# Merged stores of the x parts, and weight preparation and attention issued in other steps, in a linear-attention and two-MoE kernel

## The chip, the cores and the metric

One core of a Trainium2 chip runs the whole program in one launch. The metric is device time in microseconds (us), the median of three runs. The engines are named as in the profile: PE (TensorE; its weight loads are PEld), DVE (VectorE), ACT (ScalarE), POOL (GpSimd) and SP (SyncE), which here only issues transfers.

## What is computed

All data are float32. `B, H, S, D = 4, 8, 576, 64`; there are 2304 tokens and the model width is 512.

```python
kv = einsum('bhsd,bhse->bhde', k, v)
o = einsum('bhsd,bhde->bhse', q, kv)
o = o / sqrt(mean(o * o, -1) + 1e-06) * g_norm
x = o.transpose(0, 2, 1, 3).reshape(2304, 512)
h = x @ moe_w_in                      # 512 x 2048
x = (h * sigmoid(h)) @ moe_w_out      # 2048 x 512
a, b = x @ moe2_w_a, x @ moe2_w_b     # 512 x 1536 each
out = (a * b) @ moe2_w_out            # 1536 x 512
```

## The kernel before

**Numbers.** A matrix that goes into TensorE is split into a high part, which is a cast on ACT, and a low part, source minus high, on DVE (`halve`, L436). A product is three matmuls: high by high, high by low, low by high.

**Blocks and visits.** Tokens are worked in six blocks of 384 (`TB`), so a moving tile is 128x384. The list `VISITS` (L42) gives the first MoE layer its order: the hidden tiles (16 per block) are passed through in nine visits. Visits 0 to 4 take blocks 0 and 1 in plain steps, one hidden tile each, numbered g = 0 to 31. A plain step multiplies into a bank `hp`, has ACT apply the gate (L418) and the cast `gh` (L364), DVE the low part `gl` (L369), and then multiplies the hidden tile of the step before into the four output banks `x1p` (L380). After that come the side jobs of the step: `at(g, ...)` enters one, `at(-g, ...)` one between gate and low part, `soon` one before the gate's step.

**Units.** Blocks 2 and 3, and later 4 and 5, are worked in pairs by a scheme of seven products in place of eight (`PRODUCTS`, L51; `seven`, L661): the x of the two blocks is combined into seven parts, `X_PARTS` = B11, T2, T3, B21, T1, T4, B22, and the weights into seven combinations. Visits 5 and 7 are eight such units each (`unit`, L803); a unit makes four hidden tiles, forms its sums `u` (L678, L681) and `h` (L827) on DVE from the banks X_h, Y_h, V_h and Z_h, and has two `x1_mm` of earlier tiles in it. `at_unit(b, u, n, ...)` hangs a side job behind product n of unit u. Visits 6 and 8 (16 steps each, from `P2A` = g 48 and from `base[8]` = g 80) only multiply the second block's stored hidden tiles into the output banks: casts `gh`, low parts `gl` and 12 matmuls per step. Then 18 iterations of the same kind make the second MoE layer.

**Preparation.** `combine` (L449) makes the seven parts of x for a pair of blocks and one kt, with high and low part of each; for the second layer they go to `xcd` in DRAM, high and low by one store each, from half pages of [128, 384] (`half_page`), the blocks having been loaded by `last_blocks` (L1007) into two pages. `prepare` (L497) does the same for one pair of matrices of w_a or w_b: `load`; `scale` (two ACT operations, L305); `first_half` and `second_half` (decoding, L311, L317, L324 on DVE, and the cast of `a`); `add` (the low part of `a`, then four sums s1, s3, s2, s4, L545 to L548); `high` (casts of `s_0`, `s_1` and `m`, L437); `low` (their low parts, L438). `flush` then gives the stores to `wd` to SP. Twelve pairs (n = 0 to 11, w_a and w_b in turn) are spread over the units of blocks 2 and 4, the last over visit 8.

**Order.** The order in which the program issues is the order in which each engine works; an instruction that waits holds all that is behind it on its engine. SP issues every transfer, also in order. Most tiles are of one size and rotate through 37 buffers, the pages (`NPAGE`), so a new tile waits for the last use of an earlier one.

**Attention.** For blocks 2 and 3, `kv_pair` and `attend` are entered by the table at L925 to L935: `turn_q` transposes (L159, DVE), `stage_b` (L220, PE), the norm, and `stage_f` into `xf` (L915, ACT).

```python
for f, h in zip(steps, (0, 1, 2, 5, 5, 7)):
    at_unit(*slot(b, h0 + h), f)
```

Of the kernel before, what the change touches and what calls it, by code (L numbers as in the profile page):

```python
# [8 lines left out]
F32 = mybir.dt.float32  # L9
F32R = mybir.dt.float32r  # L10
# [50 lines left out]
def tile_linattn_moe_moe2(ctx: ExitStack, tc: tile.TileContext, q, k, v, g_norm,  # L61
                          w_in, w_out, w_a, w_b, w_out2, out):
    nc = tc.nc
    B, H, S, D = q.shape
# [28 lines left out]
    def page(shape, dt, name):  # L93
        return sb.tile(shape, dt, tag="page", bufs=NPAGE, name=name)
# [4 lines left out]
    def mid(shape, dt, name):  # L99
        return sb.tile(shape, dt, tag="mid", bufs=5, name=name)  # L100
# [245 lines left out]
    acc, part, gg = {}, {}, {}  # L346
# [88 lines left out]
    def halve(hi, lo, src, *stores):  # L435

        return (lambda: nc.scalar.copy(hi, src),  # L437
                lambda: nc.vector.tensor_sub(lo, src, hi.bitcast(F32)),  # L438
                *[lambda to=to, t=t: nc.sync.dma_start(to, t.bitcast(F32)) for to, t in stores])
# [9 lines left out]
    def combine(d, kt, place, blocks=None, keep=None, home=None):  # L449

        st, wait = {}, {}

        def new(name):
            st[name] = place([P, TB], F32, f"{name}_{d}_{kt}")
            return st[name]

        def get():
            for n in range(2):  # L460
                for r in range(2):
                    st[f"B{r + 1}{n + 1}"] = (blocks or (lambda n, r: part[2 * d + n][:, 2 * r + kt, :]))(n, r)

        def hi(name):
            h = home(name, f"h{name}_{d}_{kt}") if home else place([P, TB], F32R, f"h{name}_{d}_{kt}")
            low = home(name, f"l{name}_{d}_{kt}") if home else st[name].bitcast(F32R)
            i = X_PARTS.index(name)
            if keep is None:
                to = xcd[d, i, :, :, kt, :]
                first_, *wait[name] = halve(h, low, st[name], (to[:, 0], h), (to[:, 1], low))  # L470
            else:
                keep[i, 0, kt], keep[i, 1, kt] = h, low
                first_, *wait[name] = halve(h, low, st[name])
            first_()

        def lo(name):
            rest, *put_ = wait.pop(name)
            rest()
            if blocks:
                stores.extend(put_)  # L480
            else:
                for f in put_:
                    f()

        def sub(to, of, by, into=None):
            t = st[into] if into else place([P, TB], F32, f"{to}_{d}_{kt}")
            nc.vector.tensor_sub(t, st[of], st[by])
            st[to] = t

        return [(get, lambda: hi("B11"), lambda: sub("T1", "B12", "B11")), (lambda: hi("T1"), lambda: lo("B11")),  # L490
                (lambda: sub("T3", "B22", "B12", "B12"),), (lambda: hi("T3"), lambda: sub("T2", "B22", "T1")),
                (lambda: hi("B22"), lambda: lo("T1")), (lambda: hi("T2"), lambda: lo("T3")),
                (lambda: lo("B22"),), (lambda: sub("T4", "B21", "T2"),),
                (lambda: hi("B21"), lambda: lo("T2")), (lambda: hi("T4"), lambda: lo("B21")),
                (lambda: lo("T4"),), ()]
# [286 lines left out]
    hw, hx, xf, g1 = {}, {2: {}, 4: {}}, {}, {}  # L782
# [103 lines left out]
    base = []  # L886
    n = 0
# [5 lines left out]
    def at(g, fn, *args):  # L893
        side.setdefault(g, []).append(lambda: fn(*args))
# [27 lines left out]
    def at_unit(b, u, n, fn, *args):  # L922
        inner.setdefault((b, u, n), []).append(lambda: fn(*args))

    for b, g0s in ((2, (12, 14, 16, 18)), (3, (20, 22, 24, 26))):  # L925
        at(g0s[0] - 4, load_kvt, b)
        for g0, p in zip(g0s, (0, 2, 1, 3)):
            at(g0 - 3, load_kv, b, p)
            at(g0, kv_pair, b, p)
    for (j, p), g0 in zip([(2, 0), (2, 2), (3, 0), (3, 2), (2, 1), (2, 3), (3, 1), (3, 3)],  # L930
                          (12, 14, 16, 18, 20, 22, 24, 25)):
        at(g0 - 5, load_q_blocks, j, p)
        at(g0 - 2, turn_q, j, p)
        at(g0, attend, j, p)
        at(-(g0 + 1), norm_mul, j, p)  # L935
        at(g0 + 3, stage_f, j, p)

    P2A = base[6]
# [15 lines left out]
    def half_page(shape, dt, name):  # L954

        if not halves:
            t = page([P, 2, TB], F32R, name)
            halves.extend((t[:, 1], t[:, 0]))
        t = halves.pop()
        return t if dt == F32R else t.bitcast(dt)  # L960

    def home(part_, name):

        if part_ == "B11":
            return first.tile([P, TB], F32R, tag="qb", bufs=4, name=name)
        return half_page([P, TB], F32R, name)

    def x_parts(b, kt, places):
        todo = []

        def parts(n):
            if not todo:
                todo.extend(combine(f"h{b}", kt, mid, lambda n, r: xf[b, 2 * r + kt][:, n], hx[b], home))
            for f in todo[n]:
                f()

        for n, g in enumerate(places):
            at(g, parts, n)
# [10 lines left out]
    def slot(b, h):  # L989
        return (b,) + divmod(min(h, 7 * NF1 // 2 - 1), 7)  # L990

    for n in range(2 * NPAIR):
        load, steps = prepare(("wa", "wb")[n % 2], n // 2, n <= 7)
        if n == 2 * NPAIR - 1:
            at_unit(4, 7, 3, load)
            for i, f in enumerate(steps):
                at(base[8] + 1 + i, f)
            continue
        b, h0 = (2, 7 * (n + 2)) if n < 3 else (4, 7 * (n - 3))
        if h0 == 0:  # L1000
            at(P2A + 14, load)
        else:
            at_unit(*slot(b, h0 - 5), load)
        for f, h in zip(steps, (0, 1, 2, 5, 5, 7)):
            at_unit(*slot(b, h0 + h), f)

    def last_blocks(d, kt):  # L1007

        t = [page([P, 2, TB], F32, f"b_{kt}_{r}") for r in range(2)]
        for r in range(2):  # L1010
            for n in range(2):
                nc.sync.dma_start(t[r][:, n], x1d[2 * d + n, :, 2 * r + kt, :])
        return lambda n, r: t[r][:, n]

    for i in range(3):
        at(P2A + i, lambda: put())
    for u in (5, 6, 7):
        for n in range(7):
# [1 line left out]
    for kt in range(2):  # L1020
        todo = []

        def blocks0(kt=kt, todo=todo):
            todo.extend(combine(0, kt, half_page, last_blocks(0, kt)))

        def parts0(n, todo=todo):
            for f in todo[n]:
                f()

        at_unit(2, 5 + kt, 6, blocks0)  # L1030
        for n in range(12):
            at_unit(2, 6 + kt, 1 + n // 2, parts0, n)

    made = {}

# [8 lines left out]
    for u in range(6):  # L1044
        g0 = (7, 10, 14, 18, 22, 25)[u]
# [165 lines left out]
    with tc.manual_schedule():  # L1211
# [63 lines left out]
        todo, late = [], {}  # L1275
        for n, (d, p) in enumerate(seq):
            new = 0 < n < NPAIR
            m = n % NPAIR
            if 1 <= m <= 4 and n < 2 * NPAIR:

                kt, h = divmod(m - 1, 2)
                if h == 0:
                    late[kt] = combine(d + 1, kt, half_page, late.pop("blocks"))
                todo = late[kt][6 * h:6 * h + 6]
            products(d, p, (lambda: x1_mm(*prev)) if n == 0 else None,
                     decode_out(p, 0) if 0 < n < NPAIR else [])
            if n % NPAIR == NPAIR - 1 and n + 1 < len(seq):
                for i in range(7):
                    load_x(d + 1, i)
            free_pairs(n, False)  # L1290
            load_pairs()
            if n > 0:
                more = [(f,) for f in decode_out(p, 1)] if new else []
                if todo:
                    more = [(tuple(more[i]) if more else ()) + tuple(todo[i]) for i in range(6)]
                out_mm(n - 1, more)
                todo = []
                free_pairs(n - 1, True)
# [36 lines left out]
```

## Time and profile before

| | |
|---|---|
| runs, us | 868.41, 868.54, 867.34; median 868.41 |
| the profiled execution, us | 866.76; its span 865.0 |
| PE busy | 850.8 us, 98% of the span |
| PEld | 807.4 us, 93% |
| DVE | 622.2 us, 72% |
| ACT | 347.8 us, 40% |
| POOL | 52.6 us, 6% |
| bytes over the span | 230.03 MB, 266 GB/s |

All stages are PE work with other engines beside it, so the table says only that the time is PE's. What a change of order does is read where PE waits, on the time line of that place. Matmuls are pipelined: a row that gives 1.20 us for six matmuls of 384 columns is followed by the next 1.04 us after its start, and an instruction of DVE or ACT likewise overlaps the next by 0.05 to 0.1 us. The distance of two starts is therefore the price of an instruction, and its duration the time until others can use its result.

### The profile page before, as it was taken

The page shows a single profiled execution, that of the slowest core. Times are in us where ns is not written, and L with a number is a line of the kernel's source. Part 1 is how long each engine was busy: PE and PEld are TensorE (multiplying, and loading weights), DVE is VectorE, ACT ScalarE, POOL GpSimd, SP SyncE. Part 2 cuts the span into 40 slices and gives each one's busy share as a digit, 9 for nine tenths or more (in the row PEclk, how much of TensorE's full clock was granted, in tenths as well). Part 3 has the DMA queues.
Part 4 walks back from the last instruction along what each step waited for, and adds up shares of the span by engine and source line. Part 5 has one row for each costly group of instructions (what it writes and reads, how often), then busy time and mean ns, then how long its engine had stood idle before and what let it go on. Part 6 is the DMA issues. An engine that isn't in the chain of part 4 may idle for free.

```text
span 865.0 us, 13734 instructions
## 1 busy us (share of the span) xinstructions
PE 850.8 (98%) x4966; PEld 807.4 (93%) x4967; DVE 622.2 (72%) x1191; ACT 347.8 (40%) x708; POOL 52.6 (6%) x73
## 2 busy tenths in 40 slices
PE   7999999999999999999999999999999999999998
PEld 5799999999998999999999999999999999999996
DVE  4879989777956779989746788876576665545555
ACT  4666765544545456556522533221412211221110
POOL 5430111100000500000000000000000000000000
PEclk9999999999999999999999999999999999999999
DMA  9985886189986659999999998496688475755001
GB/s 276 372 222 160 258 244 234 66 312 405 408 315 183 190 218 336 405 404 385 369 405 417 388 336 333 152 379 242 238 305 276 135 292 200 292 219 195 1 0 74
DMA packets 127972, 230.03 MB, mean 266 GB/s; under 512 B 41504, under 2 KB 87072, under 8 KB 127904
## 3 DMA queue, kind: packets, MB, share of 16 engines
q1 hardware_dynamic: 127904, 229.15, 73.7%
q8 instruction: 39, 0.64, 0.3%
q14 instruction: 29, 0.24, 0.1%
HBM read 160.17 MB, written 68.94 MB: 265 GB/s over the span
## 4 chain that ended last, share of the span: by engine, by line
PE 83%; DMA 9%; DVE 4%; ACT 2%; issue 1%; SPq 1%; POOL 0%; DVEq 0%; ACTq 0%
PE x1p L380 18%; PE op L865 17%; PE hp L354 8%; PE Z_b L671 4%; PE X_b L671 4%; PE V_b L671 4%; PE Z_a L671 4%; PE X_a L671 4%; PE V_a L671 4%; DMA wd<-a_wa 2%; PE V_h L671 2%; PE X_h L671 2%; PE Y_b L671 2%; PE Y_a L671 2%; PE Z_h L671 2%; PE ao L220 2%
## 5 line engine op out<-in xcount | busy, mean ns | idle before, releaser
L380 PE MATMUL x1p<-gh,wo 128*128 128x384 f32 x768 | 195.0, 337 | 0.3 <-ACT gh L364 0.3
L380 PEld LDWEIGHTS x1p<-gh,wo 128*128 128x128 f32 x768 | 138.0, 188 | 0.6 <-ACT gh L364 0.6
L380 PE MATMUL x1p<-gl,wo 128*128 128x384 f32 x384 | 127.9, 337 | 1.1 <-DVE gl L369 1.1
L865 PE MATMUL op<-wp,ab 128*128 128x512 f32 x360 | 83.4, 390 | 0.0
L728 ACT CAST ab<-a 128x384 fp32r<-128x384 f32 x72 | 37.0, 514 | 115.0 <-DVE a L722 58.3
L865 PEld LDWEIGHTS op<-wp,ab 128*128 128x128 f32 x360 | 67.4, 188 | 13.7
L369 DVE TENSOR_TENSOR gl<-g,gh 128x384 fp32r<-128x384 f32 x96 | 54.0, 563 | 30.6 <-ACT gh L364 30.4
L380 PEld LDWEIGHTS x1p<-gl,wo 128*128 128x128 f32 x384 | 71.9, 188 | 2.0 <-DVE gl L369 2.0
L873 DVE TENSOR_TENSOR o<-op,o 128x512 f32<-128x512 f32 x90 | 60.4, 686 | 16.6 <-PE op L865 16.6
L865 PE MATMUL op<-w,ab 128*128 128x512 f32 x288 | 66.9, 390 | 0.0
L865 PEld LDWEIGHTS op<-w,ab 128*128 128x128 f32 x288 | 53.9, 188 | 10.9
L364 ACT CAST gh<-g 128x384 fp32r<-128x384 f32 x96 | 49.2, 513 | 22.4 <-PE x1p L380 20.6
L354 PE MATMUL hp<-xh,wi 128*128 128x384 f32 x256 | 52.7, 345 | 0.4 <-ACT xh L260 0.3
L238 POOL TENSOR_TENSOR rr<-ss,nhalf 128x6 f32<-128x6 f32 x24 | 34.4, 1435 | 229.4 <-DVE ss L233 229.3
L354 PEld LDWEIGHTS hp<-xh,wi 128*128 128x128 f32 x256 | 43.8, 188 | 1.4 <-ACT xh L260 1.0
L671 PE MATMUL X_a<-xc,wp 128*128 128x384 f32 x216 | 43.8, 337 | 0.0
L671 PE MATMUL Z_a<-xc,wp 128*128 128x384 f32 x216 | 43.4, 335 | 0.1
L671 PE MATMUL V_a<-xc,wp 128*128 128x384 f32 x216 | 43.3, 335 | 0.0
L671 PE MATMUL Z_b<-xc,wp 128*128 128x384 f32 x216 | 43.3, 335 | 0.0
L671 PE MATMUL V_b<-xc,wp 128*128 128x384 f32 x216 | 43.3, 335 | 0.0
L671 PE MATMUL X_b<-xc,wp 128*128 128x384 f32 x216 | 43.3, 334 | 0.0
L732 DVE TENSOR_TENSOR ab<-a,ab 128x384 fp32r<-128x384 f32 x72 | 39.8, 553 | 2.2 <-ACT ab L728 0.6
(172 smaller groups left out, 1551.6 us busy)
## 6 DMA issues: line engine op xcount, KB each, us to landing
wp<-wd SPq DMA_DIRECT2D x114, 512.0 KB, 6.5
hw<-hsd SPq DMA_DIRECT2D x32, 512.0 KB, 8.5
xc<-xcd SPq DMA_DIRECT2D x21, 768.0 KB, 8.5
hw<-had SPq DMA_DIRECT2D x16, 768.0 KB, 8.4
raw_wi<-in_moe_w_in_dram SPq DMA_DIRECT2D x16, 512.0 KB, 7.0
raw_wo<-in_moe_w_out_dram SPq DMA_DIRECT2D x16, 512.0 KB, 6.0
hsd<-hs SPq DMA_DIRECT2D x16, 512.0 KB, 5.0
raw_wa<-in_moe_w_a_dram SPq DMA_DIRECT2D x12, 512.0 KB, 7.8
```

The costliest lines, as they stand in the source:

```text
L220: nc.tensor.matmul(o[a:e, i], t[:, i * P + a:i * P + e], kvc[bb, p], start=True, stop=True)
L238: nc.gpsimd.tensor_tensor(r, rms[j, p], nhalf, op=ALU.pow)
L354: nc.tensor.matmul(o, w[wp][:, kt * P:(kt + 1) * P], x[key][:, kt, :], start=(n == 0), stop=(n == 3 * KD - 1))
L364: nc.scalar.copy(gh, src)
L369: nc.vector.tensor_sub(gl, src, gh.bitcast(F32))
L380: nc.tensor.matmul(acc[vi][c], w[wp][:, c * P:(c + 1) * P], gg[vi, s][g], start=(s == s0 and i == 0), stop=(s == s1 - 1 and i == 2))
L671: nc.tensor.matmul(b[bank], w(name, wq, kt), x(i, xq, kt), start=(fresh and k == 0), stop=(k == 5), skip_group_check=True)
L728: nc.scalar.copy(o[:, 0], t)
L732: low = lambda t=t, o=o: nc.vector.tensor_sub(o[:, 1], t, o[:, 0].bitcast(F32))
L865: nc.tensor.matmul(o, ab[d, p, f, n][:, g, ts], wp[p, 7 + f][:, wq * DM:(wq + 1) * DM], start=(k == 0), stop=(k == 5))
L873: nc.vector.tensor_add(t, o, t)
```

## The change

1. In `combine`, high and low of a part now share one page of [128, 2, 384], the block itself is loaded into the low half, and one store of 384 KB takes the place of two of 192 KB: 42 stores to `xcd` for 84. Four pages per kt are taken by the loads, where two were, and three more by the sums; seven in all both ways.
2. Attention of blocks 2 and 3 stands at g = 11, 13, ... 25 (before 12, 14, ... 24, 25), and its transposes and loads move with it; the k-v products of block 2 at 11 to 17, of block 3 at 19 to 25.
3. The first pair of w_a (n = 0) is loaded at g = 22 and prepared in visits 3 and 4: scale 24, halves 25 and 26, add and high 30, low 31 (before in units 2 and 3 of block 2). Pairs 1 to 3 are in units 2 to 4 of block 2, pairs 4 to 10 in units 0 to 6 of block 4 (before 3 to 10 in units 0 to 7). The last pair starts one step earlier in visit 8, at `base[8]`.
4. The last four groups of the parts for d = 0, kt = 1 leave unit 7 of block 2 and are done in the first four steps of visit 6.

No arithmetic is added or taken away: PE, DVE, ACT and POOL have the same number of instructions as before. The diff, cut:

```diff
 def combine(d, kt, blocks, keep=None, home=None):
-    first_, *wait[name] = halve(h, low, st[name], (to[:, 0], h), (to[:, 1], low))
+    t = both_[name]
+    first_, *wait[name] = halve(t[:, 0], t[:, 1], st[name], (xcd[d, i, :, :, kt, :], t))
...
-    for b, g0s in ((2, (12, 14, 16, 18)), (3, (20, 22, 24, 26))):
+    for b, g0s in ((2, (11, 13, 15, 17)), (3, (19, 21, 23, 25))):
...
-                          (12, 14, 16, 18, 20, 22, 24, 25)):
+                          range(11, 27, 2)):
...
-    load, steps = prepare(("wa", "wb")[n % 2], n // 2, n <= 7)
+    load, steps = prepare(("wa", "wb")[n % 2], n // 2, n <= 8)
     if n == 2 * NPAIR - 1:
-        at_unit(4, 7, 3, load)
+        at_unit(4, 7, 2, load)
         for i, f in enumerate(steps):
-            at(base[8] + 1 + i, f)
+            at(base[8] + i, f)
         continue
-    b, h0 = (2, 7 * (n + 2)) if n < 3 else (4, 7 * (n - 3))
+    if n == 0:
+        at(22, load)
+        for f, g0 in zip(steps, (24, 25, 26, 30, 30, 31)):
+            at(g0, f)
+        continue
+    b, h0 = (2, 7 * (n + 1)) if n < 4 else (4, 7 * (n - 4))
...
-    t = [page([P, 2, TB], F32, f"b_{kt}_{r}") for r in range(2)]
+    t = {}
     for r in range(2):
         for n in range(2):
-            nc.sync.dma_start(t[r][:, n], x1d[2 * d + n, :, 2 * r + kt, :])
+            t[n, r] = page([P, 2, TB], F32R, f"b_{d}_{kt}_{n}{r}")
+            nc.sync.dma_start(t[n, r][:, 1].bitcast(F32), x1d[2 * d + n, :, 2 * r + kt, :])
...
-    for n in range(12):
+    for n in range(12 - 4 * kt):
         at_unit(2, 6 + kt, 1 + n // 2, parts0, n)
+    for n in range(12 - 4 * kt, 12):
+        at(-(P2A + n - 8), parts0, n)
```

**First place: the steps g = 30 and 31 and the first unit of blocks 2 and 3.** `g_4_15` and `gh_4_15` are gate and cast of the last plain step, `hB..`, `hT..` parts of x for the unit. ACT before:

```order
L437 CAST hB22_h2_1_2257<-xf_2_3_1989 128x384
L437 CAST hT2_h2_1_2260<-T2_h2_1_2222 128x384
L418 ACTIVATE g_4_15_2279<-hp_4_15_2266 128x384
L364 CAST gh_4_15_2281<-g_4_15_2279 128x384
L437 CAST hB21_h2_1_2299<-xf_2_3_1989 128x384
L437 CAST hT4_h2_1_2302<-T4_h2_1_2264 128x384
L676 COPY u2_h_2_0_2313<-X_h_2_0_2306 128x384
```

ACT now:

```order
L437 CAST hB22_h2_1_2273<-xf_2_3_1959 128x384
L437 CAST hT2_h2_1_2276<-T2_h2_1_2238 128x384
L437 CAST s_0_wa0_2283<-s_0_wa0_2283 128x512
L437 CAST s_1_wa0_2284<-s_1_wa0_2284 128x512
L437 CAST m_wa1_1967<-m_wa1_1967 128x256
L418 ACTIVATE g_4_15_2305<-hp_4_15_2292 128x384
L364 CAST gh_4_15_2307<-g_4_15_2305 128x384
L437 CAST hB21_h2_1_2325<-xf_2_3_1959 128x384
L437 CAST hT4_h2_1_2328<-T4_h2_1_2280 128x384
L680 COPY u2_h_2_0_2342<-X_h_2_0_2335 128x384
```

Three casts of the weight pair stand between the part T2 and the gate of step 31. DVE in the same place, before:

```order
L438 TENSOR_TENSOR hB22_h2_1_2257<-xf_2_3_1989,hB22_h2_1_2257 128x384
L487 TENSOR_TENSOR T4_h2_1_2264<-xf_2_3_1989,T2_h2_1_2222 128x384
L369 TENSOR_TENSOR gl_4_15_2285<-g_4_15_2279,gh_4_15_2281 128x384
L438 TENSOR_TENSOR hT2_h2_1_2260<-T2_h2_1_2222,hT2_h2_1_2260 128x384
L438 TENSOR_TENSOR hB21_h2_1_2299<-xf_2_3_1989,hB21_h2_1_2299 128x384
L438 TENSOR_TENSOR hT4_h2_1_2302<-T4_h2_1_2264,hT4_h2_1_2302 128x384
L678 TENSOR_TENSOR u2_h_2_0_2313<-Y_h_2_0_2319,u2_h_2_0_2313 128x384
L755 TENSOR_TENSOR hs_0_6_2327<-wi_12_1541 128x512
```

DVE now, right behind the low part of `a` (`a_wa0`):

```order
L549 TENSOR_TENSOR s_0_wa0_2283<-m_wa1_1967 128x256
L550 TENSOR_TENSOR s_1_wa0_2284<-m_wa0_1965,m_wa1_1967 128x256
L551 TENSOR_TENSOR s_0_wa0_2283<-s_0_wa0_2283,m_wa0_1965 128x256
L552 TENSOR_TENSOR s_1_wa0_2284<-m_wa0_1965,s_0_wa0_2283 128x256
L369 TENSOR_TENSOR gl_4_15_2311<-g_4_15_2305,gh_4_15_2307 128x384
L438 TENSOR_TENSOR hT2_h2_1_2276<-T2_h2_1_2238,hT2_h2_1_2276 128x384
L438 TENSOR_TENSOR hB21_h2_1_2325<-xf_2_3_1959,hB21_h2_1_2325 128x384
L438 TENSOR_TENSOR hT4_h2_1_2328<-T4_h2_1_2280,hT4_h2_1_2328 128x384
L438 TENSOR_TENSOR s_0_wa0_2283<-s_0_wa0_2283 128x512
L438 TENSOR_TENSOR s_1_wa0_2284<-s_1_wa0_2284 128x512
L438 TENSOR_TENSOR m_wa1_1967<-m_wa1_1967 128x256
L682 TENSOR_TENSOR u2_h_2_0_2342<-Y_h_2_0_2349,u2_h_2_0_2342 128x384
```

Five operations of the pair have come ahead of `gl_4_15`, and three low parts ahead of the first unit's sum `u2`.

**Second place: DVE at the end of unit 7 of block 2, around `gl_2_15`.** Before:

```order
L827 TENSOR_TENSOR h_2_7_10_3332<-V_h_2_7_3229,u2_h_2_7_3197 128x384
L438 TENSOR_TENSOR T2_0_1_3268<-T2_0_1_3268,hT2_0_1_3296 128x384
L438 TENSOR_TENSOR b_1_1_3185<-b_1_1_3185,hB21_0_1_3352 128x384
L827 TENSOR_TENSOR h_2_7_01_3363<-Z_h_2_7_3299,u2_h_2_7_3197 128x384
L369 TENSOR_TENSOR gl_2_15_3365<-g_2_15_3334,gh_2_15_3336 128x384
L438 TENSOR_TENSOR hT2_0_1_3296<-hT2_0_1_3296,hB21_0_1_3352 128x384
```

Now:

```order
L438 TENSOR_TENSOR b_0_1_11_3217<-b_0_1_11_3217 128x384
L491 TENSOR_TENSOR T4_0_1_3348<-b_0_1_01_3215,T2_0_1_3294 128x384
L831 TENSOR_TENSOR h_2_7_10_3356<-V_h_2_7_3256,u2_h_2_7_3226 128x384
L831 TENSOR_TENSOR h_2_7_01_3381<-Z_h_2_7_3324,u2_h_2_7_3226 128x384
L369 TENSOR_TENSOR gl_2_15_3383<-g_2_15_3358,gh_2_15_3360 128x384
L159 STREAM_TRANSPOSE qT_4_0_3386<-qb_4_0_3237 128x384
L369 TENSOR_TENSOR gl_3_0_3395<-g1_2_0_2417,gh_3_0_3393 128x384
```

The low parts of T2 and B21 (`T2_0_1`, `b_1_1`) have left the place ahead of `h_2_7_01`.

**Third place: ACT in the first steps of visit 8.** `gh_5_s` is the cast of step s, `m_wb10` and `m_wb11` the last weight pair. Before:

```order
L364 CAST gh_5_1_4986<-g1_4_0_3965 128x384
L305 ACTIVATE m_wb10_5006<-raw_wb10_4878 128x512
L305 ACTIVATE m_wb11_5008<-raw_wb11_4880 128x512
L364 CAST gh_5_2_5014<-g1_4_0_3965 128x384
L364 CAST gh_5_3_5041<-g1_4_0_3965 128x384
L437 CAST a_wb5_5057<-m_wb10_5006 128x512
L364 CAST gh_5_4_5066<-g1_4_1_4226 128x384
L584 ACTIVATE m_w20_5092<-raw_w20_4982 128x512
L364 CAST gh_5_5_5094<-g1_4_1_4226 128x384
L437 CAST s_0_wb5_5083<-s_0_wb5_5083 128x512
L437 CAST s_1_wb5_5084<-s_1_wb5_5084 128x512
L437 CAST m_wb11_5008<-m_wb11_5008 128x256
```

Now:

```order
L305 ACTIVATE m_wb10_4966<-raw_wb10_4871 128x512
L305 ACTIVATE m_wb11_4968<-raw_wb11_4873 128x512
L364 CAST gh_5_1_4976<-g1_4_0_3984 128x384
L364 CAST gh_5_2_5003<-g1_4_0_3984 128x384
L437 CAST a_wb5_5019<-m_wb10_4966 128x512
L364 CAST gh_5_3_5032<-g1_4_0_3984 128x384
L364 CAST gh_5_4_5059<-g1_4_1_4245 128x384
L437 CAST s_0_wb5_5049<-s_0_wb5_5049 128x512
L437 CAST s_1_wb5_5050<-s_1_wb5_5050 128x512
L437 CAST m_wb11_4968<-m_wb11_4968 128x256
L588 ACTIVATE m_w20_5081<-raw_w20_4972 128x512
L364 CAST gh_5_5_5083<-g1_4_1_4245 128x384
```

The two scales have passed `gh_5_1`, the cast of `a` has passed `gh_5_3`, and the three casts of the sums have passed `gh_5_5` and `m_w20`.

## Rows read from the trace of the kernel before

**Rows 1.** Busy time over the whole span, by engine.

```profile
PE 850.8 (98%) x4966; PEld 807.4 (93%) x4967; DVE 622.2 (72%) x1191; ACT 347.8 (40%) x708; POOL 52.6 (6%) x73
```

**Rows 2.** Waits of PE: us in total, times, longest us.

```profile
PE x1p L380 <- DVE gl L369: 1.1, 1, 1.1
...
PE V_h L671 <- DVE u_h L681: 0.7, 1, 0.7
PE ao L220 <- ACT xf L915: 0.7, 1, 0.7
```

**Rows 3.** Time line of PE at 155 us: start, us, instruction, idle before.

```profile
155.74 0.94 PE L220 MATMUL ao<-kvc,qT 128*128 128x128 f32 x6 [0.67 <-ACT xf L915]
```

**Rows 4.** Time line of PE, 414 to 427 us.

```profile
417.12 0.51 PE L380 MATMUL x1p<-gh,wo 128*128 128x384 f32 x2
...
425.86 0.62 PE L380 MATMUL x1p<-gh,wo 128*128 128x384 f32 x2 [0.26 <-ACT gh L364]
```

**Rows 5.** Time line of DVE at 83 us.

```profile
82.77 0.57 DVE L159 STREAM_TRANSPOSE qT<-qb 128x384 f32<-128x384 f32 x1
```

**Rows 6.** Time line of DVE, 270 to 278 us.

```profile
269.81 0.56 DVE L487 TENSOR_TENSOR b<-b,b 128x384 f32<-128x384 f32 x1 [1.02 <-DMA b<-x1d]
...
275.85 0.56 DVE L438 TENSOR_TENSOR b<-b,hB 128x384 fp32r<-128x384 f32 x1 [1.08 <-ACT hB L437]
...
276.80 0.55 DVE L369 TENSOR_TENSOR gl<-g,gh 128x384 fp32r<-128x384 f32 x1
```

**Rows 7.** Time line of DVE, 176 to 192 us.

```profile
180.07 0.55 DVE L487 TENSOR_TENSOR T_h<-xf,T_h 128x384 f32<-128x384 f32 x1
182.35 0.56 DVE L369 TENSOR_TENSOR gl<-g,gh 128x384 fp32r<-128x384 f32 x1 [1.73 <-ACT gh L364]
...
185.52 0.56 DVE L678 TENSOR_TENSOR u_h<-Y_h,u_h 128x384 f32<-128x384 f32 x1 [1.20 <-PE Y_h L671]
...
190.99 0.55 DVE L827 TENSOR_TENSOR h<-Z_h,u_h 128x384 f32<-128x384 f32 x1
```

**Rows 8.** Time line of ACT, 176 to 186 us.

```profile
181.28 0.49 ACT L418 ACTIVATE g<-hp 128x384 f32<-128x384 f32 x1 [2.30 <-PE hp L354]
```

**Rows 9.** Time line of DVE, 412 to 427 us, weight pairs.

```profile
412.59 1.29 DVE L438 TENSOR_TENSOR s_wa<-s_wa 128x512 fp32r<-128x512 f32 x2
...
417.69 0.56 DVE L369 TENSOR_TENSOR gl<-g,gh 128x384 fp32r<-128x384 f32 x1 [0.97 <-ACT gh L364]
...
422.68 0.68 DVE L438 TENSOR_TENSOR a_wb<-m_wb,a_wb 128x512 fp32r<-128x512 f32 x1
423.28 0.42 DVE L545 TENSOR_TENSOR s_wb<-m_wb 128x256 f32<-128x256 f32 x1
...
423.95 0.42 DVE L547 TENSOR_TENSOR s_wb<-s_wb,m_wb 128x256 f32<-128x256 f32 x1
```

**Rows 10.** Time line of ACT, 413 to 427 us.

```profile
415.62 0.52 ACT L364 CAST gh<-g 128x384 fp32r<-128x384 f32 x1
416.03 1.23 ACT L305 ACTIVATE m_wb<-raw_wb 128x512 f32<-128x512 f32 x2
...
424.75 0.66 ACT L584 ACTIVATE m_w<-raw_w 128x512 f32<-128x512 f32 x1 [2.87 <-DMA raw_w<-in_moe_w_out_dram]
425.31 0.50 ACT L364 CAST gh<-g 128x384 fp32r<-128x384 f32 x1
425.71 1.14 ACT L437 CAST s_wb<-s_wb 128x512 fp32r<-128x512 f32 x2
```

**Rows 11.** Time line of PE, 183 to 193 us.

```profile
191.59 1.31 PE L671 MATMUL Z_h<-hB_h,hw 128*128 128x384 f32 x6
```

**Rows 12.** Time line of PE, 270 to 278 us.

```profile
277.40 0.44 PE L380 MATMUL x1p<-gl,wo 128*128 128x384 f32 x1 [1.15 <-DVE gl L369]
```

**Rows 13.** Time line of SP at 175 us.

```profile
174.98 1.26 SPq L778 DMA_DIRECT2D hsd<-hs  x2
```

**Rows 14.** DMA issues of the whole span: xcount, KB each, us to landing.

```profile
hsd<-hs SPq DMA_DIRECT2D x16, 512.0 KB, 5.0
```

More of the change, by code (lines that the diff above doesn't have):

```diff
@@ L447, in flush, with combine @@
         fresh_.clear()
[L449 to L457, printed above, removed]
+    def combine(d, kt, blocks, keep=None, home=None):
+        st, both_, wait = {}, {}, {}
         def get():
@@ L461, in get @@
                 for r in range(2):
-                    st[f"B{r + 1}{n + 1}"] = (blocks or (lambda n, r: part[2 * d + n][:, 2 * r + kt, :]))(n, r)
+                    name = f"B{r + 1}{n + 1}"
+                    t = blocks(n, r)
+                    if keep is None:
+                        both_[name] = t
+                        t = t[:, 1].bitcast(F32)
+                    st[name] = t
         def hi(name):
-            h = home(name, f"h{name}_{d}_{kt}") if home else place([P, TB], F32R, f"h{name}_{d}_{kt}")
-            low = home(name, f"l{name}_{d}_{kt}") if home else st[name].bitcast(F32R)
             i = X_PARTS.index(name)
             if keep is None:
-                to = xcd[d, i, :, :, kt, :]
-                first_, *wait[name] = halve(h, low, st[name], (to[:, 0], h), (to[:, 1], low))
+                t = both_[name]
+                first_, *wait[name] = halve(t[:, 0], t[:, 1], st[name], (xcd[d, i, :, :, kt, :], t))
             else:
+                h, low = (home(name, f"{c}{name}_{d}_{kt}") for c in "hl")
                 keep[i, 0, kt], keep[i, 1, kt] = h, low
@@ L478, in lo, with sub @@
             rest()
-            if blocks:
-                stores.extend(put_)
-            else:
[L482 to L486, printed above, removed]
+            stores.extend(put_)
+        def sub(to, of, by, into=None):
+            if into:
+                t = st[into]
+                if keep is None:
+                    both_[to] = both_[into]
+            elif keep is None:
+                both_[to] = page([P, 2, TB], F32R, f"{to}_{d}_{kt}")
+                t = both_[to][:, 1].bitcast(F32)
+            else:
+                t = mid([P, TB], F32, f"{to}_{d}_{kt}")
             nc.vector.tensor_sub(t, st[of], st[by])
@@ L972, in parts @@
             if not todo:
-                todo.extend(combine(f"h{b}", kt, mid, lambda n, r: xf[b, 2 * r + kt][:, n], hx[b], home))
+                todo.extend(combine(f"h{b}", kt, lambda n, r: xf[b, 2 * r + kt][:, n], hx[b], home))
             for f in todo[n]:
@@ L1007, in last_blocks @@
     def last_blocks(d, kt):
-        t = [page([P, 2, TB], F32, f"b_{kt}_{r}") for r in range(2)]
+        t = {}
         for r in range(2):
             for n in range(2):
-                nc.sync.dma_start(t[r][:, n], x1d[2 * d + n, :, 2 * r + kt, :])
-        return lambda n, r: t[r][:, n]
-    for i in range(3):
+                t[n, r] = page([P, 2, TB], F32R, f"b_{d}_{kt}_{n}{r}")
+                nc.sync.dma_start(t[n, r][:, 1].bitcast(F32), x1d[2 * d + n, :, 2 * r + kt, :])
+        return lambda n, r: t[n, r]
+    for i in range(5):
         at(P2A + i, lambda: put())
@@ L1023, in blocks0 @@
         def blocks0(kt=kt, todo=todo):
-            todo.extend(combine(0, kt, half_page, last_blocks(0, kt)))
+            todo.extend(combine(0, kt, last_blocks(0, kt)))
         def parts0(n, todo=todo):
@@ L1282, in tile_linattn_moe_moe2 @@
                 if h == 0:
-                    late[kt] = combine(d + 1, kt, half_page, late.pop("blocks"))
+                    late[kt] = combine(d + 1, kt, late.pop("blocks"))
                 todo = late[kt][6 * h:6 * h + 6]
```

## The prediction

> **What bounds the kernel now.** The busy shares come first [rows 1]: PE works 850.8 of 865.0 us. The change takes no matmul away, so it can win only what PE loses in waits, and lose wherever it makes PE wait anew. The list of PE's waits [rows 2] says how much there is to win: besides waits of the first 50 us, there is one of 1.1 for the low part `gl`, one of 0.7 for a sum `u` of a unit and one of 0.7 for `xf`. Everything else is under half a microsecond. So I looked up where these stand on the time line of PE, which engine's last instruction ended them, and then, in the order of the changed program, which engine queues get something put in front of an instruction that PE waits for. The average shares of DVE (72%) and ACT (40%) decide nothing: in the places below both are free before and after, and late in between. The measurement can tell about 0.2% from no change, here 1.7 us; all terms below are around that size, which is the main thing to know about this change.
>
> The sum is made against the profiled execution, 866.76 us (span 865.0). It stands 1.65 below the median of the runs shown, 868.41; the same difference goes onto the median.
>
> **Attention at every second step.** The eight steps of attention keep all instructions; only two of them were in adjoining steps (24 and 25). There PE waits 0.67 us [rows 3], because the transposes of the last head pair need a bank that ACT empties into `xf`. With two steps between them the bank is emptied one step earlier, so I take this wait away: with the slower first matmuls behind a stop (0.62 for two where 0.51 is usual, [rows 4]) it is worth 0.8. It is not a term of its own, because PE meets the next stall 35 us on and what it is early by is lost there; it goes into the next calculation as a shift of 0.8.
>
> In steps 9 to 12 each of two low parts gets a transpose ahead of it on DVE, one also a small reduction. A transpose takes 0.57 us [rows 5], and one instruction of DVE starts 0.47 after the last (three starts from 275.85 to 276.80, [rows 6]). Both low parts have some slack, so the bounds are 0 and 2 x 0.5 = 1.0; I take **+0.2**, near the lower end, since one instruction for one instruction of slack leaves little.
>
> **The first w_a pair in visits 3 and 4.** This is the largest term. Its load, scales and decoding fill gaps of ACT and DVE in steps 24 to 26; DVE waits 1.73 us for a cast in the later of these plain steps [rows 7], and the gate on ACT 2.30 for PE [rows 8]. I cost that at nothing. But `add` and `high` hang on step 30, and ACT then has three casts that need DVE's sums, ahead of the gate of step 31. Step by step:
>
> - T4, the last instruction of DVE before the pair, starts at 180.07 [rows 7]; less 0.8 and plus its 0.47 the pair starts at 179.74. The low part of `a` takes 0.60 (422.68 to 423.28), the third sum starts 0.67 after the first and takes 0.42 [rows 9]: s2 is done at 179.74 + 0.60 + 0.67 + 0.42 = 181.43.
> - ACT casts `s_0` and `s_1` (1.14 for both, 1.04 by the start of what follows, [rows 10]) and `m`, half as wide, about 0.35: the gate starts at 181.43 + 1.4 = 182.8, where it started at 181.28 [rows 8].
> - DVE's `gl_4_15` follows the gate by 1.07 (181.28 to 182.35): 183.87. DVE idles for two microseconds before it. Three low parts of x follow, so the next instruction starts at 183.87 + 4 x 0.47 = 185.75. Then come the low parts of `s_0`, `s_1`, `m`: 1.20 for the first two and 0.34, to 187.29 [rows 9].
> - Only then the unit's first sum `u2`, which before started at 185.52 after 1.20 us of idle time [rows 7]. That idle time is all the slack there is: from there to `h` at 190.99 DVE has one instruction behind the other, 5.47 us. So `h` starts at 192.76, and PE's last product of the unit, which before followed at 191.59 [rows 11], 0.60 later, at 193.4.
>
> That is **+1.8** against before, with the 0.8 of attention already used up. Bounds: 0.9 if the sums or low parts overlap better than the pitches say and the shift is kept in part, 2.6 if the shift does not come.
>
> The units lose what visits 3 and 4 gain, but in units 2 to 7 of blocks 2 and 3 PE waits only at the two places of the next paragraph; emptier engines buy nothing elsewhere. Pairs 1 to 3 and 4 to 10 keep their distances inside a unit and are costed at 0; their cover is DVE's idle time in a unit.
>
> **Parts of x out of unit 7.** At 276 us PE waits 1.15 for `gl_2_15` [rows 12]. DVE starts it at 276.80, because ahead of it a low part of B21 waits 1.08 for its cast on ACT [rows 6], which stands there behind gate and cast of another tile. Both low parts leave this place, so `gl_2_15` follows the sum `h` directly, about 275.4, and is done in time for PE at about 276.1. With the slower matmuls behind the stop the wait is worth **-1.3** (bounds -1.4 and -0.5). The parts go into the first four steps of visit 6, where ACT and DVE have one cast and one low part each per 2.1 us besides attention; cost 0.
>
> **One store for two, four pages for two.** No wait of PE ends on a store to `xcd`, and the consumers load them over 100 us later. The 42 stores fewer shorten SP's queue ahead of the four loads of the second blocks, whose landing ends DVE's wait of 1.02 at 269.81 [rows 6]. But SP reaches those loads only after the low part of B21 of the kt before, which DVE makes at the same place as before. Four pages must be free where two had to be; all four had their last use before that. I take **-0.1**, between +1 (a page late) and -0.5 (PE's share of that wait gone).
>
> **The last pair a step earlier in visit 8.** On ACT its scales, 1.23 for two [rows 10], go ahead of `gh_5_1`: from 415.62 to 416.74, done at 417.25, where PE's step starts at 417.12 [rows 4]. `gl_5_1` then runs from 417.28 to 417.83 and is wanted at 417.46: PE waits 0.4. The rest of the chain starts behind `gl_5_1` at 417.28 and not behind `gl_5_2` at 417.69 [rows 9], so it is only 0.4 early: third sum done at 423.95 + 0.42 - 0.4 = 424.0. Now three casts (1.4) stand ahead of `m_w20`, which waits for its load until 424.75 [rows 10], and `gh_5_5`: 425.4, plus 0.55 for `m_w20`, gives 425.9 for the cast that ran at 425.31. PE was already late there (0.26 of idle time at 425.86, [rows 4]). Later by 0.6, with the earlier 0.4 contained in it: **+0.5** (bounds 0 and 1.0).
>
> **Sum:** 0.2 + 1.8 - 1.3 - 0.1 + 0.5 = +1.1 us. 866.76 + 1.1 = 867.9 for an execution like the profiled one, 868.41 + 1.1 = **869.5** against the median: no change that a measurement can tell.
>
> **Rivals.**
>
> *The pair does not hold the unit (chance 0.20).* If DVE makes up the delay between `u2` and `h`, or ACT's casts come sooner, the 1.8 go and attention's 0.8 stay: 868.41 + 0.2 - 0.8 - 1.3 - 0.1 + 0.5 = 866.9; if the wait of 0.7 for `u` near 395 us [rows 2] goes too, since pair 7 now stands in another unit, 866.2 or a little less. For it: DVE idles two microseconds ahead of `gl_4_15`, so little is wrong. Against: engines work in order, and nothing idles between 185.52 and 190.99.
>
> *A page comes late (0.15): slower.* `s_0` of the first pair takes the page of `hs_0_5`, a tile of combined weights of visit 4. Its store is issued at 174.98 [rows 13], and such stores land 5.0 after issue [rows 14]: 180.0, where the first sum is wanted at 179.74 + 0.60 = 180.34. It has 0.3 us to spare. Everything behind it in the chain above moves one for one. A landing 0.9 late (5.9 after issue) already makes the kernel slower by over 0.2%; 7.5 us after issue gives 869.5 + 2.2 = 871.7. For it: the load of the pair is ahead of that store in SP's queue. Against: it was issued more than five steps earlier.
>
> *The merged stores bring the blocks sooner (0.08).* DVE's wait of 1.02 goes, and PE's part of it, 0.5: 869.0. The Trainium skill, page "DMA: Bandwidth & Descriptors", section "Anatomy of one DMA", gives about 2.0 us per transfer besides its bytes, for another way of issue than SP's here; by it each pair merged saves that once, the blocks would come up to 2 us sooner, and the sum would be this rival's. No row before shows a merged store.
>
> **How the numbers follow.** The forecast has 0.57, with its bounds some 868 to 871; a fifth of it lies above 870.1 and a small part below 866.7, the marks of 0.2%. The first rival lies about three quarters below 866.7, the second nearly all above 870.1, the third between. Faster 0.21, same 0.53, slower 0.26. The range, 866.2 to 871.8, takes in the forecast's bounds and most of both rivals.
>
> **What would show it.** In the profile after: no wait of `ao` for `xf` near 155; a wait of PE at the first unit's last Z_h near 191, on DVE's `h`, of some 2.5 us in all with `gl` idle before; no wait for `gl_2_15` near 277; a wait of `x1p` for `gl_5_1` near 418. It is wrong if PE's time from 150 to 200 is not lost at that unit, if the wait near 277 stays, or if `add` is seen waiting for a DMA.

## The result and the profile after

| | before | changed |
|---|---|---|
| median, us (6 runs each) | 868.28 | 873.72 |
| lowest to highest | 866.95 to 868.55 | 872.69 to 874.81 |
| ratio, 95% interval | | 1.0067, 1.0054 to 1.008 |
| profiled execution; span | 866.76; 865.0 | 874.81; 873.0 |
| mean granted clock | 1.000 | 0.996 |

The change made the kernel slower by 5.4 us (4.7 to 6.9 by the interval). Forecast were 869.5 and a range up to 871.8. The two profiled executions lie 8.0 apart, more than the medians, since the one of before lies 1.5 below its median and the one after 1.1 above; sums from the traces are therefore larger than those of the medians.

One correction to the description ahead of the prediction: a job entered with `at(-g)` comes first among the side jobs behind the step's multiplications, and one entered with `soon` between the cast and the low part. No term hung on that.

The waits of PE after (us in total, times, longest), to be held against [rows 2]:

```profile
PE V_h L675 <- DVE u_h L685: 4.1, 4, 1.9
PE Z_h L675 <- DVE h L831: 2.4, 1, 2.4
...
PE X_h L675 <- ACT u_h L680: 0.9, 2, 0.5
PE xtp L256 <- DVE xn L243: 0.9, 1, 0.9
...
PE Y_h L675 <- DVE hT_h L438: 0.5, 1, 0.5
...
PE x1p L380 <- DVE gl L369: 0.2, 1, 0.2
```

The waits for `xf` (0.7) and for `gl_2_15` (1.1) are gone as forecast. In their place stand waits in the units: 7.4 us for the sums and 0.5 for a low part of x, where before there were 0.9 for sums (0.7 of them [rows 2]). Where the longest of them are, windows of the trace after show (length, then busy us and count for PE, PEld, DVE, ACT and POOL, granted clock, share and rate of the DMA):

```profile
175.00:183.00 8.00, 8.00 (x48) 8.00 (x47) 4.46 (x10) 4.28 (x10) 0.00 (x0) 1.00 1.03 350
183.00:190.00 7.00, 6.06 (x34) 5.42 (x33) 3.67 (x8) 1.84 (x5) 0.00 (x0) 1.00 0.78 303
190.00:196.00 6.00, 1.92 (x10) 1.27 (x8) 5.74 (x13) 0.80 (x3) 0.00 (x0) 0.96 0.67 272
196.00:202.00 6.00, 5.78 (x18) 5.78 (x19) 3.42 (x7) 3.28 (x7) 0.00 (x0) 0.50 1.03 362
202.00:208.00 6.00, 6.00 (x36) 6.00 (x35) 4.01 (x9) 1.37 (x3) 0.00 (x0) 0.97 1.01 372
```

The same stretch of the kernel before, 175 to 200, was full:

```profile
175.00:200.00 25.00, 25.00 (x144) 24.75 (x144) 18.74 (x40) 10.36 (x22) 0.00 (x0) 1.00 0.87 329
```

The first unit of blocks 2 and 3 is where the time went, the place of the forecast's largest term, and it cost in two ways. PE stood four times between 183 and 196.3; and from 196 to 202 it was busy at the lower of its two levels (granted clock 0.50, 1.2 GHz): 18 matmuls in 6 us, where 36 ran in the 6 us after. That second part alone is 18 matmuls at half rate, an estimated 3 us.

One measure serves for all kernels below, the time of the first two units: on PE's time line, from the first X_h product of the first unit to that of the third. It was 183.16 to 204.20 before, 21.0 us, and is 181.63 to 211.61 now, 30.0 us.

What PE waited for, in the same unit. PE:

```profile
188.23 1.31 PE L675 MATMUL X_h<-hB_h,hw 128*128 128x384 f32 x6 [0.42 <-ACT u_h L680]
...
192.43 1.34 PE L675 MATMUL V_h<-hT_h,hw 128*128 128x384 f32 x6 [1.85 <-DVE u_h L685]
196.22 2.29 PE L675 MATMUL Z_h<-hB_h,hw 128*128 128x384 f32 x6 [2.44 <-DVE h L831]
```

DVE (compare [rows 7]):

```profile
178.54 0.55 DVE L491 TENSOR_TENSOR T_h<-xf,T_h 128x384 f32<-128x384 f32 x1
179.01 0.68 DVE L438 TENSOR_TENSOR a_wa<-m_wa,a_wa 128x512 fp32r<-128x512 f32 x1
179.61 0.42 DVE L549 TENSOR_TENSOR s_wa<-m_wa 128x256 f32<-128x256 f32 x1
...
183.15 0.56 DVE L369 TENSOR_TENSOR gl<-g,gh 128x384 fp32r<-128x384 f32 x1 [1.99 <-ACT gh L364]
...
187.83 0.56 DVE L438 TENSOR_TENSOR hT_h<-T_h,hT_h 128x384 fp32r<-128x384 f32 x1 [3.19 <-ACT hT_h L437]
...
189.85 0.55 DVE L682 TENSOR_TENSOR u_h<-Y_h,u_h 128x384 f32<-128x384 f32 x1
190.62 1.29 DVE L759 TENSOR_TENSOR hs<-wi 128x512 f32<-128x512 f32 x2 [0.23 <-PE Z_h L675]
...
195.62 0.55 DVE L831 TENSOR_TENSOR h<-Z_h,u_h 128x384 f32<-128x384 f32 x1
```

ACT (compare [rows 8]) and SP:

```profile
180.73 1.14 ACT L437 CAST s_wa<-s_wa 128x512 fp32r<-128x512 f32 x2 [2.46 <-DVE s_wa L551]
181.78 0.40 ACT L437 CAST m_wa<-m_wa 128x256 fp32r<-128x256 f32 x1
182.09 0.48 ACT L418 ACTIVATE g<-hp 128x384 f32<-128x384 f32 x1
...
187.28 0.51 ACT L437 CAST hT_h<-T_h 128x384 fp32r<-128x384 f32 x1 [3.76 <-DMA wd<-a_wa]
```

```profile
180.55 0.38 SPq L439 DMA_DIRECT2D wd<-a_wa  x1
```

Up to `gl_4_15` the chain runs as forecast: casts, gate, 1.99 us of idle time on DVE. Then comes something that no term had: the cast of the part T4 waits 3.76 us on ACT, because it writes into the page that held `a` of the weight pair, and the store of that page, issued at 180.55, has only landed at 187.26, 6.7 us later. DVE's low part of T4 waits 3.19 behind it, and `u` starts at 189.85, not at 187.3. Then `hs`, the combined weights, waits too, with PE's Z product as its releaser: its page is that of weights (`hw_2_0_1`, by the order in which this program hands out its pages) which that very product reads last. In the kernel before, the same tile took a page of `xf` whose last uses were over by then.

### The profile page after: what moved, and what is told of

Read it like the earlier page. It is cut to its first block, busy times and chain, and to the rows that moved or that the text cites. A ratio compares the mean times of both kernels' runs of the same rounds, so it can differ in the third digit from the quotient of the medians.

```text
span 873.0 us, 13652 instructions
## 1 busy us (share of the span) xinstructions
PE 855.2 (98%) x4967; PEld 809.3 (93%) x4967; DVE 621.5 (71%) x1191; ACT 347.6 (40%) x708; POOL 52.8 (6%) x73
## 5 line engine op out<-in xcount | busy, mean ns | idle before, releaser
L380 PEld LDWEIGHTS x1p<-gl,wo 128*128 128x128 f32 x384 | 71.8, 188 | 2.2 <-DVE gl L369 2.1
L675 PE MATMUL V_h<-hT_h,hw 128*128 128x384 f32 x192 | 39.2, 338 | 4.1 <-DVE u_h L685 4.1
```

What stands on the lines that cost most here:

```text
L380: nc.tensor.matmul(acc[vi][c], w[wp][:, c * P:(c + 1) * P], gg[vi, s][g], start=(s == s0 and i == 0), stop=(s == s1 - 1 and i == 2))
L675: nc.tensor.matmul(b[bank], w(name, wq, kt), x(i, xq, kt), start=(fresh and k == 0), stop=(k == 5), skip_group_check=True)
```

## The experiments

Theory A: pages are short, tiles in the first unit wait for them, and the clock is granted lower behind the stop. Theory B, the forecast's: the order alone, three casts ahead of the gate. Theory C: the merged stores. The kernels were timed in three groups, each beside the kernel before, whose median was 868.29, 868.49 and 868.33; the ratios are against that.

**The weight pairs as before**, all else as changed: the diff's hunk on the pairs undone.

> The changed kernel with the schedule of the weight pairs (first pair in units, twelve pairs spread as before, last pair a step later) put back; merged stores, attention at every second step and the moved parts stay. Theory A (in the first unit ACT waits for a page that the stored first pair held, then the clock is granted lower) and theory B (three casts ahead of the gate of step 31 alone) both put the loss at the pair: 866.5 to 868.5 us, no wait at the first unit. Theory C (merged stores and block pages make the loss): still 870 or more.

Measured: 865.17, ratio 0.9964 (0.9952 to 0.9977). The new schedule of the pairs is what costs, by 8.5 us against the changed kernel (873.72 - 865.17); the rest is a gain, 1.3 more than the range of theories A and B had. PE takes 21.0 us for the first two units, as before the change. Theory C falls.

**The pair alone** on the kernel before: that hunk only.

> The kernel before with only the new schedule of the weight pairs. Theory A: the first unit loses 6 to 9 us as in the changed kernel, 874 to 876 in all. Theory B: 870 to 871. Theory C: 868 to 869.

Measured: 876.53, ratio 1.0093 (1.008 to 1.0107): 8.2 us, half a microsecond above theory A's range and far above B's. The first unit shows the same long stops as the changed kernel (1.85 and 2.47 us), and the first two units take 29.1 us.

**The store of `a` held back**, so that T4 takes another page:

```diff
 def add():
-    rest()
+    sub, *put_ = wait.pop(0)
+    sub()
+    held.extend(put_)
...
 def low():
+    fresh_.extend(held)
```

> The changed kernel, only the store of the first pair's a is issued with the stores of its sums, so that the part T4 gets another page. Theory A: ACT's wait of 3.8 us for that store goes, PE loses 2 to 3 us at the first unit instead of 6.4, the granted clock stays at 1.00 there, and the time falls by 4 to 6 us to 868 to 870. Theory B: the order of casts and gate is unchanged, so the time stays within 1 us of the changed kernel, 873 to 874.5.

Measured: 879.0, ratio 1.0123 (1.0109 to 1.0136): neither. DVE in the first unit:

```profile
187.37 0.55 DVE L690 TENSOR_TENSOR u_h<-Y_h,u_h 128x384 f32<-128x384 f32 x1
195.53 1.29 DVE L767 TENSOR_TENSOR hs<-wi 128x512 f32<-128x512 f32 x2 [7.61 <-DMA wd<-a_wa]
```

ACT's wait is gone and `u` starts at 187.37, the forecast's time. But the next tile, `hs_0_6`, now takes the page of `a` and waits 7.61 us for the held store. The wait was moved from one tile to another: the pages are short, whoever comes next pays. PE stands 7.32 us for `u`, and the first two units take 33.8 us.

**`a` in another pool** (`six`), so that no page waits for its store:

```diff
-    o = page([P, 2, DM], F32R, f"a_{kind}{p}")
+    o = (six if (kind, p) == ("wa", 0) else page)([P, 2, DM], F32R, f"a_{kind}{p}")
```

> The changed kernel, only the tile a of the first pair lies in the pool of six instead of a page, so that nothing in the first unit takes a page that waits for its store. Page theory: ACT's wait of 3.8 us and the 7.6 us of the held store are both gone, the first sum u starts at 187.3 as forecast, PE loses 2 to 3.5 us at the first unit and keeps the higher clock: 867 to 870. Order theory (the three casts alone): 873 to 874, no change.

Measured: 874.54, ratio 1.0064 (1.0051 to 1.0076): no change, as if theory B held. DVE shows that it doesn't:

```profile
187.23 0.55 DVE L682 TENSOR_TENSOR u_h<-Y_h,u_h 128x384 f32<-128x384 f32 x1
190.59 1.29 DVE L759 TENSOR_TENSOR hs<-wi 128x512 f32<-128x512 f32 x2 [2.81 <-PE Z_h L675]
```

`u` is on time, and `hs` waits 2.81 for the page that PE's Z product frees, up to the same moment as in the changed kernel (190.59 and 190.62). T4's page was the first wait and not the last; the pool was short by more than that one page. Of the two, the page of `hs_0_6` sets the time: without T4's wait the first two units still take 28.9 us, 1.1 less than in the changed kernel.

**Two pages relieved** (e9 below): also `s_0` of the first pair in that pool. T4 and `hs_0_6` get the pages that they had before.

```diff
-    s.append((six if roomy and h else page)([P, 2, DM], F32R, f"s_{h}_{kind}{p}"))
+    s.append((six if roomy and h or (kind, p) == ("wa", 0) else page)(
+        [P, 2, DM], F32R, f"s_{h}_{kind}{p}"))
```

> The changed kernel with a and s_0 of the first pair in the pool of six, so that T4 and the combined weights hs_0_6 of the first unit get the pages that they had before. Page theory (pages were one or two short, so that whatever DVE or ACT does next waits for a page): the waits for pages are gone, u starts at 187.3, h at 192.8, PE loses 2.6 us at the first unit as forecast and keeps its clock: 867 to 870. Order theory (casts ahead of the gate make all of the loss): no change, 873 to 874.5.

Measured: 868.73, ratio 1.001 (1.0 to 1.002), 5.0 below the changed kernel. DVE and PE in the first unit:

```profile
178.82 0.55 DVE L491 TENSOR_TENSOR T_h<-xf,T_h 128x384 f32<-128x384 f32 x1
...
186.85 0.55 DVE L682 TENSOR_TENSOR u_h<-Y_h,u_h 128x384 f32<-128x384 f32 x1
187.32 1.28 DVE L759 TENSOR_TENSOR hs<-wi 128x512 f32<-128x512 f32 x2
...
192.31 0.55 DVE L831 TENSOR_TENSOR h<-Z_h,u_h 128x384 f32<-128x384 f32 x1
```

```profile
192.91 1.32 PE L675 MATMUL Z_h<-hB_h,hw 128*128 128x384 f32 x6 [1.71 <-DVE h L831]
```

```profile
196.00:202.00 6.00, 6.00 (x36) 6.00 (x36) 4.71 (x10) 2.30 (x6) 0.00 (x0) 1.00 1.04 406
```

This is the forecast's chain to a hundredth: from T4 to `u` 8.03 us (forecast 187.29 - 179.27 = 8.02), to `h` 5.46 (5.47), to PE 0.60 (0.60). PE waits 0.52 and 1.71, and the clock stays at 1.00. The first two units take 23.7 us, 2.6 more than before: the forecast's 1.8 with the 0.8 of attention that it counted as used up. So theory A holds, and the order is worth what the forecast said, no more.

**Pages relieved and the gate first**: `high` to step 31, `low` into the second half of the first unit, steps (24, 25, 26, 30, 31, 33).

> As e9, and high goes to step 31, behind the gate, low to the second half of the first unit. Page theory: the 1.8 us that the order costs go too, 865.5 to 867.5, no stop of over 0.8 us at the first unit. Order theory: also 865.5 to 867.5; together with e9 it gives the share of the order.

Measured: 872.43, ratio 1.005 (1.0034 to 1.0065): missed. DVE:

```profile
185.47 0.56 DVE L682 TENSOR_TENSOR u_h<-Y_h,u_h 128x384 f32<-128x384 f32 x1 [0.96 <-PE Y_h L675]
...
188.10 0.69 DVE L759 TENSOR_TENSOR hs<-wi 128x512 f32<-128x512 f32 x1 [1.49 <-DMA wd<-a_wa]
...
202.44 0.69 DVE L759 TENSOR_TENSOR hs<-wi 128x512 f32<-128x512 f32 x1 [2.95 <-DMA hsd<-hs]
```

The order's cost is gone: `u` waits for PE again, as before the change. But the second half of the combined weights of the first two units now waits 1.49 and 2.95 us. These halves (`hs_1_6`, `hs_1_7`) lie in the pool of six, into which `a` and `s_0` had been moved: `hs_1_6` takes the buffer of `a`, `hs_1_7` that of `hs_1_6`, and neither store had landed. The relief had moved the shortage into the other pool. The first two units take 26.4 us. That the order's cost can be had back without a buffer that is late was not shown.

**The pair earlier**: add, high and low at steps 27, 27, 28.

> The changed kernel with add, high and low of the first pair at steps 27, 27, 28 instead of 30, 30, 31. Theory A and theory B: neither the casts nor the page are in the way of the first unit, 866.5 to 868.5 us. Theory C: 870 or more, with what is lost still lost after the first unit.

Measured: 871.56, ratio 1.0035 (1.0021 to 1.0049): missed; 2.2 below the changed kernel, 3.3 above the one before. The wait of PE that is new:

```profile
PE x1p L380 <- DVE x L408: 2.7, 1, 2.7
```

It stands between visits 3 and 4: casts ahead of the gate delay `gl`, behind which DVE empties the four output banks. The order's cost had moved to a place where it counts more: PE reaches the first unit 4.9 us later than with the pairs as before (165.7 us behind its first `hp` product, for 160.8), and the first two units then take 21.5. T4's cast still waits 1.72 us for the store, with no wait of PE behind it.

**Attention alone**, and **attention with the moved parts**, on the kernel before:

> The kernel before with only the attention of blocks 2 and 3 at every second step. Theory: the wait of 0.84 at 155 us goes, nothing else: 867.2 to 867.8. Rival (PE loses it again at the next wait): 868.1 to 868.5.

> The kernel before with attention at every second step and the last four groups of parts moved out of unit 7, with stores and pages as before. If the merged stores and their four block pages cost time: below the changed kernel with the pairs put back (865.2), 863.5 to 864.7. If they cost nothing: 865.2 to 866.3.

Measured: 866.68, ratio 0.9981 (0.997 to 0.9991), and 864.96, ratio 0.9958 (0.9946 to 0.9971). Both are gains. The first is half a microsecond better than its theory's range; the second lies between its two ranges, so that it decides nothing on the merged stores. It is the fastest kernel of this study, level with the one with pairs as before (865.17).

**The merged stores alone**:

> The kernel before with only the merged stores and the block pages of combine. If they cost: 869.3 to 870.3, with DVE waiting longer for the block loads in units 6 and 7. If not: 868 to 868.6.

Measured: 866.91, ratio 0.9982 (0.9972 to 0.9993). The median fell by 1.6, against both expectations, but its profile doesn't show where: the span is 864.8 against 865.0 in an execution of before that was itself 1.5 below its median, and PE's wait for a `u` near 269 us is new (0.85). On top of attention and parts they bring nothing (865.17 against 864.96, from two groups). What they are worth stays open, within 2 us.

**The last pair a step earlier**, on the first experiment:

> The changed kernel with the weight pairs put back (865.2), but the last pair a step earlier in visit 8. Theory of the forecast: 0.5 more, 865.5 to 866, PE waiting for gl of steps 1 and 5. Rival (nothing): 864.9 to 865.4.

Measured: 866.63, ratio 0.9986 (0.9975 to 0.9997), 1.5 more than without, which was timed in another group; above the forecast's range. The traces agree on the place: from PE's last Z_h product to its first X_a of the second layer, the stretch that holds visit 8, this kernel takes 38.4 us and the one without 36.8. In all the traces of this study it is 38.0 to 38.4 with the last pair earlier (eight kernels) and 36.6 to 38.2 without (six; the profiled execution of before 37.7). The direction agrees; the size lies between nothing and 1.6 by the kernel that it is held against, and is 0.3 to 0.7 against the profiled execution of before.

**`s_1` of the ninth pair out of the pages**, on attention and parts (`n <= 8` for `n <= 7`):

> The kernel before with attention at every second step and the moved parts (865.0), and s_1 of the ninth pair in the pool of six. If the stop at 391 to 395 us (1.4) is a wait of two sums for pages whose stores have not landed: 863.7 to 864.5. If not: 864.7 to 865.3.

Measured: 866.48, ratio 0.9984 (0.9969 to 0.9998): no gain on 864.96. Waits of DVE, 380 to 410 us:

```profile
DVE s_wa L545 <- DMA wd<-a_wb: 1.6, 1, 1.6
DVE s_wb L546 <- DMA wd<-a_wa: 1.5, 1, 1.5
```

Without the change (the kernel with attention and parts), the same stretch:

```profile
DVE s_wa L545 <- DMA wd<-a_wb: 1.3, 1, 1.3
DVE s_wa L546 <- DMA wd<-s_wb: 1.2, 1, 1.2
...
DVE s_wb L546 <- DMA wd<-s_wa: 0.6, 1, 0.6
```

The sum `s_1` of the ninth pair lost its wait of 1.2, and that of the next pair took the page of `a`, whose store was under way, and waits 1.5 where it had waited 0.6: once more the wait went to the next.

## Why the prediction was wrong

- **The first pair in visits 3 and 4: +1.8 forecast (2.6 with the 0.8 of attention used up), 8.9 measured in the first two units.** The order was right, to a hundredth of a microsecond, as the kernel with two pages relieved shows. The step that failed is the way from T4 to `h`, "Then come the low parts ... Only then the unit's first sum `u2`" and from there "one instruction behind the other, 5.47 us": it lets every instruction start when its engine and its data are ready, prices a wait for a page at nothing, and gives a reason for one tile alone, `s_0`. Two tiles of the pair, `a` and `s_0`, now held pages into the first unit, and T4 and `hs_0_6` had to take pages still in use: T4 that of `a` (3.76 us of ACT), `hs_0_6` that of weights which PE was reading. PE's idle time in the unit became 0.51 + 0.42 + 1.85 + 2.44 = 5.2 in place of some 2.5, and the clock fell behind it, an estimated 3 us more, for which the forecast had no term. In medians: the new schedule of the pairs alone costs 8.2, the relief of two pages gives back 5.0.
- **The rival "a page comes late"** named this mechanism and gave it 0.15, at the wrong tile. `s_0` did not wait (DVE goes from the low part of `a` at 179.01 to the first sum at 179.61 without a gap). With its 871.7 it also lacked the clock.
- **Attention: right.** The wait for `xf` is gone, and PE comes to the first unit 0.7 us sooner (in attention alone 160.9 us behind its first `hp` product, before 161.6), where 0.8 less 0.2 was taken. The median of attention alone fell by more, 1.6 (0.8 to 2.6); what the rest is, its trace does not show.
- **Parts of x out of unit 7: right.** The wait for `gl_2_15`, 1.1, is gone; from attention alone to both the median falls by 1.7, forecast 1.3.
- **One store for two: -0.1 forecast; not settled, and the wait was taken at the wrong instruction.** For the second kt DVE waits for the blocks twice, in the first subtraction (T1) and in the second (T3). The forecast had the second wait alone, 1.02 [rows 6], which stands behind a unit's sum `u`; it is gone. The first stands ahead of that `u`, and it grew. Before and now:

```profile
267.10 0.56 DVE L487 TENSOR_TENSOR hB<-b 128x384 f32<-128x384 f32 x1 [1.83 <-DMA b<-x1d]
```

```profile
275.57 0.56 DVE L491 TENSOR_TENSOR T<-b,b 128x384 f32<-128x384 f32 x1 [2.51 <-DMA b<-x1d]
```

  Together DVE waits 2.85 before, 2.51 now and 3.02 with the merged stores alone, so the blocks did not come sooner, and the rival that has them come sooner falls. But PE now waits 0.95 for the `u` behind the first subtraction, where it had no such wait. In all traces of this study that wait is 0.85 to 1.13 with merged stores and at most 0.53 without. The stores landed, by the DMA issues after:

```profile
xcd<-b SPq DMA_DIRECT2D x24, 384.0 KB, 4.5
xcd<-T SPq DMA_DIRECT2D x18, 384.0 KB, 4.8
```

  in 4.5 to 4.8 us, those of half the size before in 3.2 to 4.0. The Trainium skill, page "DMA: Bandwidth & Descriptors", section "Anatomy of one DMA", for another way of issue than SP's here, makes a doubled transfer dearer by its bytes alone, an estimated 0.45 us here by its rate; the step from 4.0 to 4.5 agrees, that from 3.2 to 4.8 is larger. No wait of PE ended on these stores before or after, so nothing that merging saves in them shows in PE's waits.
- **Pairs 4 to 10 "keep their distances": 0 forecast, no cost shown.** Some sums of these pairs take the pages of the pair before, and its stores are still under way:

```profile
395.42 0.42 DVE L549 TENSOR_TENSOR s_wb<-m_wb 128x256 f32<-128x256 f32 x1 [1.83 <-DMA wd<-a_wa]
396.93 0.43 DVE L550 TENSOR_TENSOR s_wb<-m_wb,m_wb 128x256 f32<-128x256 f32 x1 [1.09 <-DMA wd<-s_wa]
```

  In the kernel before the same waits were 0.8 and 1.0 in this stretch. But the kernel with the pairs as before, in which these pairs stand where they stood, has them grown as well:

```profile
386.73 0.42 DVE L549 TENSOR_TENSOR s_wa<-m_wa 128x256 f32<-128x256 f32 x1 [1.60 <-DMA wd<-a_wb]
388.48 0.42 DVE L550 TENSOR_TENSOR s_wa<-m_wa,m_wa 128x256 f32<-128x256 f32 x1 [1.33 <-DMA wd<-s_wb]
```

  So the move of the pairs is not what made them grow. PE's time for units 1 to 6 of blocks 4 and 5 says the same: 70.0 to 71.5 us in the seven kernels with the old places, 70.1 to 71.8 in the seven others.
- **The last pair: +0.5 forecast, direction right.** Of the waits foreseen, none is listed at `gl_5_1`; PE has one of 0.19 at 433.21, for a `gl` that stands behind the pair's sums on DVE. The size is not settled, as said above.

The forecast's sum, which has no page in it, is 869.5, close to the kernel that has the pages relieved, 868.73. That is in part luck: with the pairs as before the change gained 3.1 us (868.29 to 865.17), where the terms have 2.0 (0.2 - 0.8 - 1.3 - 0.1), and the relieved pairs cost 3.6 more (865.17 to 868.73), where they have 3.1 (0.8 + 1.8 + 0.5). The error that put the time outside the range is one omission, the pages with the clock behind them.

## What to carry to other kernels

Where tiles rotate through a fixed number of buffers, moving a stage earlier lengthens the time that its buffers are held, and the cost falls on the next allocations, whatever they belong to; so follow each allocation behind the moved work to the last use of the tile it replaces, a store's landing included (here 6.7 us from issue). A wait that is taken from one tile by giving it another buffer goes to the next tile as long as the pool is short: count buffers before moving waits. Price a stop of PE together with what its clock does behind it.

## What the runs showed of the hardware

In the changed kernel two stops of PE, 1.85 and 2.44 us idle and less than six microseconds apart, were followed by a granted clock of 0.50 (1.2 GHz) from 195.5 to 202.3 us; with two pages relieved, stops of 0.52 and 1.71 in the same unit were not, and the clock stayed at 1.00 (2.4 GHz). In the kernel with the pair earlier one stop of 2.66 was followed by 0.50 from 175.3 to 178.7, and in the one with the gate first a stop of 1.94 by 0.50 from 204.0 to 207.3. No run here tells what decides between a stop that is followed by the lower level and one that is not. The thing to remember is that the second cost came after the wait was over, on matmuls that waited for nothing, and that no list of waits shows it: the clock in a window does, or the length of the matmuls (2.29 us for the six of Z_h behind the stop of 2.44, 1.32 for the same six in the relieved kernel).
